# First token block in units of two feed-forward tiles, mean square of two blocks on VectorE, and a new load order, in a planned attention and feed-forward kernel

## The chip, the cores and the metric

The kernel runs on one core of one Trainium2 chip. The metric is the device time of one execution in microseconds (us).

## The reference

Attention with a window of 128 and four sink tokens over 4 batches x 8 heads x 768 positions x 64, and then, for the 3072 rows of 512 values, an RMS norm and a gated feed-forward layer of width 1536.

```python
def attention(q, k, v):                       # per batch and head
    scores = q @ k.T / sqrt(64)
    keep = (col < 4) | ((row - col >= 0) & (row - col < 128))
    a = softmax(where(keep, scores, -1e9))
    return a @ v

def ffn(x):                                   # x: 3072 x 512
    xn = x / sqrt(mean(x * x) + 1e-6) * rms_g
    g = xn @ w_gate                           # 512 x 1536
    return (g * sigmoid(g) * (xn @ w_val)) @ w_out
```

## The kernel before

The kernel works on 24 blocks of 128 tokens. A block passes through attention (transposes of q and k, scores, exponentials, masks, product with v), the RMS norm, and a transpose; four blocks form a group for the feed-forward layer, whose hidden width is cut into 12 tiles of 128 ("ft"). What is special here is that the program describes every operation with its needs, a priority and an estimated duration, and a small planner on the host (a list scheduler, run when the program is built) decides which engine's queue gets which operation next. Each engine then works through its own queue in that order and waits where a needed thing is not there yet.

```python
class Plan:
    LATE = 300
    def run(self):
        ...                                   # cut
        while left:                           # take the op that can start first,
            first = None                      # then the one of better priority
            for e, found in cand.items():
                for o in found:
                    ...                       # cut: ready time, PSUM banks
                    start = max(free[e], ready)
                    key = (start, o["prio"], ready, o["at"])
                    if first is None or key < first[0]:
                        first = key, e, o
            ...                               # cut: estimated end, DMA landing
            order.append((start, end, e, fn, o))
        return order
```

The settings that matter here: which loads go out in which order, how many of the first blocks get their mask from TensorE (as four matmuls of 512 columns that write a bias) and not from VectorE, from which block on the scores wait for a feed-forward unit (`GATE_FROM`), from which block on the loads wait for the scores of nine blocks earlier (`LEAD_FROM`), how many idle-time warm-up matmuls TensorE has, and how a group's columns and ft tiles are cut into units.

```python
    LOADS = "q-1 k-1 v-0 w-0-2 v-1 qkv-2 qkv-3 w-2-4 w-4-6 w-6-8 w-8-9 w-9-12 qkv-4 wo-0-6 qkv-5 wo-6-12 qkv-6 qkv-8 qkv-7"
    PE_MASKS = 2
    GATE_FROM = 6
    LEAD_FROM = 10
    WARM = 30
    CHUNKS = (4,2,2)                          # group 0: 4 column chunks, units of 4 ft
    GB_PRIO = 2000
    # ... cut
    def square(g):                            # ScalarE, with an accumulator
        ...
        nc.scalar.activation(out=sq, in_=x16, func=ACT.Square,
                             scale=1.0 / math.sqrt(DM), accum_out=T["ms", g])
    def rms(g):                               # VectorE, eight small operations
        m = small.tile([P, 1], FP32, name="m")
        nc.vector.tensor_scalar(out=m, in0=T.pop(("ms", g)), scalar1=1e-6, ..., op0=ALU.add)
        ...                                   # cut: 1/sqrt by iteration, then x * r * gb
    # ... cut
    for G in range(NG):
        for c in range(nc_):                  # token chunk
            for ft in range(0, FTN, nc_):     # nc_ ft tiles in a unit
                ffn(G, n, range(ft, ft + nc_), slice(c * w, (c + 1) * w), p0 + 10 * n)
    # ... cut
    order = plan.run()
    with tc.manual_schedule():
        for *_, fn, o in order:
            if fn is not None:
                fn()
```

The softmax here doesn't subtract the row's maximum and nothing guards it: scores larger than these inputs give would overflow.

Of the kernel before, what the change touches and what calls it, by code (L numbers as in the profile page):

```python
# [9 lines left out]
ALU = mybir.AluOpType  # L10
ACT = mybir.ActivationFunctionType
FP32 = mybir.dt.float32
BF16 = mybir.dt.bfloat16
I32 = mybir.dt.int32

P = 128
# [10 lines left out]
class Plan:  # L27
# [3 lines left out]


    LATE = 300
    HOP = {"PE": 40, "ACT": 35, "DVE": 35, "POOL": 90, "SP": 60}
    START = {"PE": 800, "ACT": 800, "DVE": 1030, "POOL": 1290, "SP": 800}

# [5 lines left out]
    def op(self, ways, needs=(), gives=(), prio=0.0, takes=(), drops=(), ring=None, work=0.0,  # L42
# [3 lines left out]
            drops=tuple(drops), ring=ring, work=work, mode=mode, at=len(self.ops), ready=0,  # L46
        ))

    def land(self, ring, first, work):


        r = self.rings
        if ring == "POOL":
            begin = max(first, r["POOL"], r["HW"])
            r["POOL"] = begin + (1.4 * work if begin < 8500 else work)
            self.loads -= 1
            return r["POOL"] + 520
        if ring == "HW":
            begin = max(first, r["HW"])
            r["HW"] = begin + (1.25 * work if begin > 2500 else work)  # L60
            return r["HW"] + 900
        begin = max(first, r["TR"], r["POOL"])
        if self.loads:
            r["POOL"] = max(r["POOL"], first) + work
            work *= 2
        r["TR"] = begin + work
        return r["TR"] + (350 if ring == "TR" else 650)

    def run(self):
        free, users = dict(self.START), {}  # L70
        self.loads = sum(o["ring"] == "POOL" for o in self.ops)
        wait = {o["at"]: set(o["needs"]) for o in self.ops}
        cand = {e: [] for e in free}
        left = len(self.ops)
        for o in self.ops:
            for t in o["needs"]:
                users.setdefault(t, []).append(o)
            if not o["needs"]:
                for e in o["ways"]:
                    cand[e].append(o)  # L80
        busy, warm, mode, order = [], False, 0, []
        while left:
            first = None
            for e, found in cand.items():
                for o in found:
                    k = len(o["takes"])
                    if k > len(self.banks):
                        continue
                    ready = o["ready"] + self.HOP[e] if o["ready"] else 0
                    if k:  # L90
                        ready = max(ready, sorted(self.banks.values())[k - 1] + 40)
                    start = max(free[e], ready)
                    key = (start, o["prio"], ready, o["at"])
                    if first is None or key < first[0]:
                        first = key, e, o
            if first is None:
                raise RuntimeError("stuck: %s" % [
                    (o["gives"], list(wait[o["at"]])) for o in self.ops if o["at"] in wait
                ][:20])
            (start, *_), e, o = first  # L100
            for x in o["ways"]:
                cand[x].remove(o)
            wait.pop(o["at"])
            left -= 1
            ns, lat, fn = o["ways"][e]
            if e == "PE":
                busy = [(a, d) for a, d in busy if a > start - 3413]
                warm = start - free[e] < 4000 and (warm or sum(d for a, d in busy) > 3000)
                ns = ns if warm else 2 * ns
                if o["mode"] != mode:  # L110
                    ns, mode = ns + 110, o["mode"]
                busy.append((start, ns if mode != 2 else 0))
                lat = ns + 180
            for s in o["takes"]:
                i = min(self.banks, key=lambda i: (self.banks[i], i))
                del self.banks[i]
                self.held[s] = i
            free[e] = start + ns
            end = start + lat
            if o["ring"] is not None:  # L120
                end = self.land(o["ring"], end, o["work"]) + self.LATE
            for s in o["drops"]:
                self.banks[self.held[s]] = end + 12
            for t in o["gives"]:
                for x in users.pop(t, ()):
                    x["ready"] = max(x["ready"], end + 12)
                    w = wait[x["at"]]
                    w.discard(t)
                    if not w:
                        for way in x["ways"]:  # L130
                            cand[way].append(x)
            order.append((start, end, e, fn, o))
        return order
# [3 lines left out]
def kernel(  # L137
# [13 lines left out]
    nc = tc.nc  # L151

    B, H, S, D = q.shape
    DM = H * D
# [8 lines left out]
    FTN = DFF // P  # L163
# [4 lines left out]
    HW = 4 * VW  # L168
# [3 lines left out]
    GROW = "SP"  # L172
    CAST_DVE = 600
    MASKS_PRIO = -5
    POOL_AT = (1,2)
    DEPTH = 8
    LOADS = "q-1 k-1 v-0 w-0-2 v-1 qkv-2 qkv-3 w-2-4 w-4-6 w-6-8 w-8-9 w-9-12 qkv-4 wo-0-6 qkv-5 wo-6-12 qkv-6 qkv-8 qkv-7"
    LOADS += "".join(f" qkv-{g}" for g in range(9, NB))
    PE_MASKS = 2
    POOL_MASK_FROM = 16  # L180
    X_DMA_FROM = 9
    QK_DMA_FROM = 8
    LD = 16
    GATE_FROM = 6
    LOAD_LEAD = 9
    LEAD_FROM = 10
    WARM = 30
    GATE_LEAD = 6
    T_LEAD = 3
    SPLIT = (0,1)  # L190
    CHUNKS = (4,2,2)
    GB_PRIO = 2000

    const = ctx.enter_context(tc.tile_pool(name="const", bufs=1))
    ld = ctx.enter_context(tc.tile_pool(name="ld", bufs=LD))
# [35 lines left out]
    T = {}  # L231
# [294 lines left out]
    def normal(g, u):  # L526
# [7 lines left out]
            in1=rden.unsqueeze(2).to_broadcast((P, 4, D)), op=ALU.mult,  # L534
        )

    def square(g):
        T["ms", g] = small.tile([P, 1], FP32, name="ms")
        sq = xpool.tile([P, DM], BF16, name="sq")
        nc.scalar.activation(  # L540
            out=sq, in_=T["x16", g].rearrange("p h d -> p (h d)"), func=ACT.Square,
            scale=1.0 / math.sqrt(DM), accum_out=T["ms", g],
        )

    def rms(g):
        m = small.tile([P, 1], FP32, name="m")
        nc.vector.tensor_scalar(
            out=m, in0=T.pop(("ms", g)), scalar1=1e-6, scalar2=None, op0=ALU.add,
        )
        y = small.tile([P, 1], FP32, name="y")  # L550
        nc.vector.tensor_scalar(
            out=y.bitcast(I32), in0=m.bitcast(I32), scalar1=-0.5,
# [94 lines left out]
    for g in range(NB):  # L647
# [41 lines left out]
        for u in range(2):  # L689
# [7 lines left out]
            else:  # L697
# [12 lines left out]
            dve(548, lambda g=g, u=u: normal(g, u),  # L710
                [("av", g, u)] + ([("xr", g - 3)] if g >= 3 else [])
                + ([("n", g - 1, u)] if g else []), [("n", g, u)], early, drops=[("av", g, u)])
        act(720, lambda g=g: square(g),
            [("n", g, 0), ("n", g, 1), "table"] + ([("ms", g - 1)] if g else []), [("ms", g)],
            early)
        dve(1745, lambda g=g: rms(g),
            [("ms", g), "gb"] + ([("xt", g - 3)] if g >= 3 else [])
            + ([("xr", g - 1)] if g else []), [("xr", g)], early)

        G = g // GB  # L720
# [32 lines left out]
    def mms(ps, w_sb, G, fts, cols):  # L753
        n = cols.stop - cols.start
        for i, ft in enumerate(fts):
            for kt in range(KTN):
# [2 lines left out]
                    rhs=T["xnt", G][:, kt, cols], start=(kt == 0), stop=(kt == KTN - 1),  # L759
                )  # L760

    def tanh(key):
        T["th", key] = spool.tile([P, 512], BF16, name="th")
        nc.scalar.activation(  # L764
            out=T["th", key], in_=BANK[("g", key)], func=ACT.Tanh, scale=0.5,
        )

    def silu(key):
        T["p1", key] = spool.tile([P, 512], BF16, name="p1")
        nc.vector.scalar_tensor_tensor(  # L770
            out=T["p1", key], in0=T.pop(("th", key)), scalar=1.0, in1=BANK.pop(("g", key)),
            op0=ALU.add, op1=ALU.mult,
        )

    def hidden(key, G, fts, cols):
        n, hk = len(fts), ("h", G, fts[0] // 4)
        if hk not in T:
            T[hk] = hpool.tile([P, 4, GN], BF16, name="hT")
        i = fts[0] % 4
        nc.vector.tensor_tensor(  # L780
            out=T[hk][:, i:i + n, cols],
            in0=T.pop(("p1", key)).rearrange("p (n c) -> p n c", n=n),
            in1=BANK.pop(("v", key)).rearrange("p (n c) -> p n c", n=n), op=ALU.mult,
        )

    def project(G, tb, i):
# [45 lines left out]
    def ffn(G, n, fts, cols, prio):  # L832
# [1 line left out]
        xs = [("xt", g) for g in range(G * GB + cols.start // P, G * GB + cols.stop // P)]  # L834
        before = [("h", keys[-3])] if len(keys) >= 3 else []
        keys.append(key)
        pe(864, lambda: mms(bank(("g", key)), wg, G, fts, cols),
           xs + [("wg", ft) for ft in fts], [("g", key)], prio, takes=[("g", key)])
        pe(864, lambda: mms(bank(("v", key)), wv, G, fts, cols),
           [("g", key)] + [("wv", ft) for ft in fts], [("u", key), ("F", G, n)], prio - 0.5,  # L840
           takes=[("v", key)])
        act(480, lambda: tanh(key), [("g", key), "table"] + before, [("th", key)])
        dve(600, lambda: silu(key), [("th", key)] + before, [("p1", key)], drops=[("g", key)])
        dve(605, lambda: hidden(key, G, fts, cols), [("p1", key), ("u", key)]
            + ([("O", G - 2, i) for i in range(GB)] if G >= 2 else []),
            [("h", key)], drops=[("v", key)])

    for G in range(NG):
# [1 line left out]
        nc_ = CHUNKS[G] if G < len(CHUNKS) else 1  # L850
        w, n = GN // nc_, 0
        for c in range(nc_):
            for ft in range(0, FTN, nc_):
                ffn(G, n, range(ft, ft + nc_), slice(c * w, (c + 1) * w), p0 + 10 * n)
                n += 1
        mine = [key for key in keys if key[0] == G]
        for tb in range(GB if G < NG - 1 else GB - 1):
# [61 lines left out]
```

## Time and profile before

| kernel before | |
|---|---|
| time, median of 3 | 246.89 us (246.82 to 247.07) |
| profiled execution | 245.98 us, span 244.3 us |
| TensorE busy | 232.6 us, 95% |
| VectorE / ScalarE busy | 183.7 / 131.2 us |

In the profile lines PE is TensorE (matmuls), PEld its weight loads, DVE VectorE, ACT ScalarE, POOL GpSimd and SP SyncE; L12 is line 12 of the kernel.

These are lines of the first two parts of the page of the kernel before: busy time of each engine, and the span in 40 slices (a digit is the busy share in tenths).

```profile
PE 232.6 (95%) x2098; PEld 147.8 (61%) x2120; DVE 183.7 (75%) x482; ACT 131.2 (54%) x276; POOL 88.8 (36%) x114
PE   4978999999999999999999999999999999999994
PEclk9999999999999999999999999999999999999999
DMA  8999999999999999999944544014311013200022
```

TensorE is full except in the first four slices, so TensorE bounds the kernel and only the start has idle TensorE time to give. DMA is full for the first half, because every q, k, v and weight has to come in.

The windows view of the kernel before gives busy time by engine for each stretch (start:end, length, then busy us and number of instructions of PE, PEld, DVE, ACT and POOL; then the granted TensorE clock, the DMA share and GB/s).

```profile
0.00:5.00 5.00, 1.88 (x11) 1.16 (x12) 2.59 (x16) 1.90 (x2) 3.79 (x10) 1.00 0.64 103
5.00:10.00 5.00, 4.45 (x35) 2.62 (x34) 0.99 (x3) 2.91 (x8) 5.00 (x7) 1.00 1.85 173
10.00:15.00 5.00, 4.12 (x63) 2.79 (x61) 4.01 (x16) 3.64 (x12) 5.00 (x7) 1.00 2.36 157
15.00:20.00 5.00, 3.58 (x62) 2.61 (x59) 4.46 (x16) 4.93 (x13) 3.31 (x6) 1.00 1.70 187
20.00:25.00 5.00, 4.81 (x92) 4.61 (x90) 4.29 (x12) 2.29 (x5) 3.33 (x5) 1.00 1.50 193
```

TensorE has 5.97 us idle in the first 20, almost nothing after that.

The timeline of TensorE of the kernel before (start, duration, what, and in brackets the idle time before it and what ended it):

```profile
4.16 1.87 PE L438 MATMUL s<-bias,idnos 128*128 128x512 bf16 x4 [2.07 <-DVE bias L273]
...
8.79 1.12 PE L399 MATMUL gb<-grow,ones 1*128 1x512 f32 x2
...
11.15 1.02 PE L438 MATMUL s<-bias,ident 128*128 128x512 bf16 x4
...
18.14 0.61 PE L757 MATMUL g<-xnt,wg 128*128 128x128 bf16 x8
19.75 0.62 PE L757 MATMUL g<-xnt,wg 128*128 128x128 bf16 x8 [1.00 <-DMA wg<-in_moe_w_gate_dram]
```

Three things are to be seen. Four mask matmuls of the same shape take 1.87 us at 4.16 and 1.02 us at 11.15, so TensorE runs at half its rate at first. The line PEclk shows 9 (of 10) throughout: it does not show this half rate. And the first feed-forward matmul comes at 18.14 and waits 1.00 us for the second gate load.

### The profile page before, as it was taken

The numbers are of one execution on the slowest core, as the hardware profiler recorded it, in microseconds if no ns is written. First come the engines' busy times: TensorE is split into PE (matmuls) and PEld (weight loads), VectorE is DVE, ScalarE is ACT, GpSimd is POOL, SyncE is SP. The second block draws the span as 40 slices with busy tenths as digits, with TensorE's granted clock in tenths as the row PEclk, the third lists the DMA queues.
The fourth block names the chain that finished last, engine by engine and source line by source line (L and its number), as shares of the span: only waits on it lengthen the run. The fifth ranks groups of instructions, "written<-read, shape, count | busy, mean of one in ns | idle before, by whom it ended". The sixth has DMA issues, their size and how long they took to land.

```text
span 244.3 us, 5510 instructions
## 1 busy us (share of the span) xinstructions
PE 232.6 (95%) x2098; PEld 147.8 (61%) x2120; DVE 183.7 (75%) x482; ACT 131.2 (54%) x276; POOL 88.8 (36%) x114
## 2 busy tenths in 40 slices
PE   4978999999999999999999999999999999999994
PEld 2557996875789765688875444444545544444443
DVE  4388979979899998899888499991299992377700
ACT  3886466778675837654537555735745521333111
POOL 8995755695444749423004200302504200000000
PEclk9999999999999999999999999999999999999999
DMA  8999999999999999999944544014311013200022
GB/s 112 172 170 195 192 188 188 156 146 174 171 196 130 156 124 179 142 216 133 149 35 107 133 107 86 3 21 108 120 34 21 4 21 107 86 3 0 0 86 86
DMA packets 111979, 27.22 MB, mean 111 GB/s; under 512 B 102097, under 2 KB 109009, under 8 KB 111954
## 3 DMA queue, kind: packets, MB, share of 16 engines
q0 software_dynamic: 80704, 13.90, 81.0%
q1 hardware_dynamic: 31106, 12.85, 27.0%
q8 instruction: 16, 0.26, 0.5%
q10 hardware_dynamic: 144, 0.13, 0.2%
q14 instruction: 9, 0.07, 0.1%
HBM read 28.31 MB, written 6.29 MB: 142 GB/s over the span
## 4 chain that ended last, share of the span: by engine, by line
PE 77%; DVE 9%; POOL 5%; DMA 4%; issue 3%; ACT 0%; POOLq 0%; DVEq 0%; ACTq 0%
PE o L790 23%; PE g L757 21%; PE v L757 21%; PE s L456 4%; DMA wg<-in_moe_w_gate_dram 4%; DVE hT L780 2%; PE av L520 2%; DVE p L770 2%; PE av L515 2%; DVE r L560 2%; POOL v L327 1%; DVE xr L564 1%; PE av L505 1%; PE o_last L808 1%; DVE x L532 1%
## 5 line engine op out<-in xcount | busy, mean ns | idle before, releaser
L757 PE MATMUL g<-xnt,wg 128*128 128x128 bf16 (+2 forms) x525 | 69.8, 282 | 1.6 <-DMA wg<-in_moe_w_gate_dram 1.2
L757 PE MATMUL v<-xnt,wv 128*128 128x128 bf16 (+2 forms) x522 | 71.0, 281 | 0.3
L764 ACT ACTIVATE th<-g 128x512 bf16<-128x512 f32 x72 | 42.9, 600 | 46.7 <-PE g L757 45.2
L790 PE MATMUL o<-wo,hT 128*128 128x512 bf16 x263 | 62.6, 379 | 1.2 <-issue 0.6
L770 DVE SCALAR_TENSOR_TENSOR p<-th,g 128x512 bf16<-128x512 bf16 x72 | 48.1, 683 | 16.6 <-ACT th L764 16.2
L757 PEld LDWEIGHTS <-wg 128*128 128x128 bf16 x528 | 43.1, 98 | 21.0 <-DMA wg<-in_moe_w_gate_dram 1.5
L757 PEld LDWEIGHTS <-wv 128*128 128x128 bf16 x528 | 42.6, 98 | 18.5 <-issue 0.8
L469 ACT ACTIVATE e<-s 128x512 bf16<-128x512 f32 (+1 forms) x104 | 48.4, 542 | 6.6 <-PE s L456 6.3
L780 DVE TENSOR_TENSOR hT<-p,v 128x512 bf16<-128x512 bf16 x72 | 47.2, 682 | 1.5 <-PE v L757 0.6
L790 PEld LDWEIGHTS <-hT 128*128 128x128 bf16 x276 | 25.6, 98 | 28.7 <-issue 1.3
L491 POOL TENSOR_SCALAR_AFFINE_SELECT e<-e 128x512 bf16<-128x512 bf16 x14 | 9.4, 680 | 61.8 <-ACT e L469 48.8
L798 ACT ACTIVATE osb<-o 128x512 f32<-128x512 f32 x23 | 13.8, 599 | 29.0 <-PE o L790 29.0
L323 POOL DMA_DIRECT2D k<-in_k_dram x23 | 20.5, 890 | 15.9 <-DMA v<-in_v_dram 7.0
L323 POOL DMA_DIRECT2D q<-in_q_dram x23 | 20.5, 893 | 13.0 <-DMA k<-in_k_dram 3.8
L327 POOL DMA_DIRECT2D v<-in_v_dram x24 | 21.3, 889 | 10.0 <-DMA q<-in_q_dram 6.0
L532 DVE TENSOR_TENSOR x<-av,rden 128x256 bf16<-128x256 f32 x48 | 20.4, 425 | 1.7
L540 ACT ACTIVATE sq<-x 128x512 bf16<-128x512 bf16 x24 | 15.2, 632 | 9.4 <-DVE x L532 9.3
L531 DVE RECIPROCAL rden<-av 128x4 f32<-128x4 f32 x48 | 8.5, 177 | 15.4 <-PE av L520 15.3
L486 DVE TENSOR_TENSOR e<-e,masks 128x1024 bf16<-128x1024 bf16 (+1 forms) x30 | 18.9, 650 | 1.0 <-ACT e L469 0.8
L564 DVE SCALAR_TENSOR_TENSOR xr<-x,r,gb 128x512 bf16<-128x512 bf16 x24 | 19.0, 790 | 0.9
L520 PE MATMUL av<-v,e 128*128 128x65 bf16 x192 | 16.9, 194 | 0.0
L515 PE MATMUL av<-v,e 128*128 128x65 bf16 x160 | 15.0, 193 | 0.0
(70 smaller groups left out, 177.2 us busy)
## 6 DMA issues: line engine op xcount, KB each, us to landing
out_dram<-osb SPq DMA_DIRECT2D x23, 256.0 KB, 2.2
v<-in_v_dram POOLq DMA_DIRECT2D x24, 128.0 KB, 10.4
q<-in_q_dram POOLq DMA_DIRECT2D x23, 128.0 KB, 10.9
k<-in_k_dram POOLq DMA_DIRECT2D x23, 128.0 KB, 10.8
wo<-in_moe_w_out_dram POOLq DMA_DIRECT2D x2, 768.0 KB, 12.0
wg<-in_moe_w_gate_dram POOLq DMA_DIRECT2D x4, 256.0 KB, 7.8
wv<-in_moe_w_val_dram POOLq DMA_DIRECT2D x4, 256.0 KB, 8.2
wg<-in_moe_w_gate_dram POOLq DMA_DIRECT2D x1, 384.0 KB, 9.4
```

The source lines that it names most:

```text
L323: nc.gpsimd.dma_start(out=T[name, g], in_=block_of(src, g))
L327: nc.gpsimd.dma_start(out=V16[b][:, t, :, 0:D], in_=block_of(v, g))
L469: nc.scalar.activation(out=T["e", g, u][:, 2 * hi:2 * hi + 2, n0:n1, :].rearrange("p x n c -> p x (n c)"), in_=ps.rearrange("p (j c) -> p ...
L515: nc.tensor.matmul(out=dest, lhsT=T["e", g - 1, u][:, x, 1, :], rhs=V16[b][:, t - 1, h, :], start=(t == 1), stop=False, skip_group_check=True,
L520: nc.tensor.matmul(out=dest, lhsT=T["e", g, u][:, x, 0, :], rhs=V16[b][:, t, h, :], start=(t == 0), stop=True, skip_group_check=True,)
L532: nc.vector.tensor_tensor(out=T["x16", g][:, 4 * u:4 * u + 4, :], in0=pvv[:, :, 0:D], in1=rden.unsqueeze(2).to_broadcast((P, 4, D)), op=AL ...
L564: nc.vector.scalar_tensor_tensor(out=T["xr", g], in0=T.pop(("x16", g)).rearrange("p h d -> p (h d)"), scalar=r[:, 3:4], in1=gb, op0=ALU.mu ...
L757: nc.tensor.matmul(out=ps[:, i * n:(i + 1) * n], lhsT=w_sb[:, kt, ft * P:(ft + 1) * P], rhs=T["xnt", G][:, kt, cols], start=(kt == 0), sto ...
L764: nc.scalar.activation(out=T["th", key], in_=BANK[("g", key)], func=ACT.Tanh, scale=0.5,)
L770: nc.vector.scalar_tensor_tensor(out=T["p1", key], in0=T.pop(("th", key)), scalar=1.0, in1=BANK.pop(("g", key)), op0=ALU.add, op1=ALU.mult,)
L780: nc.vector.tensor_tensor(out=T[hk][:, i:i + n, cols], in0=T.pop(("p1", key)).rearrange("p (n c) -> p n c", n=n), in1=BANK.pop(("v", key)) ...
L790: nc.tensor.matmul(out=BANK[("o", G, tb)], lhsT=T["h", G, ft // 4][:, ft % 4, tb * P:(tb + 1) * P], rhs=wo[:, ft, :], start=(ft == 0), sto ...
```

## The change

The intent is to let feed-forward work start earlier: the first token block works in units of two ft tiles, so that it needs only one pair of weight loads to begin; weights for ft 2-3 come before ft 0-1; both after the q, k, v of blocks 1 to 3; and the mean square plus eps of the first two blocks is one VectorE operation with an accumulator, where ScalarE's Square, its accumulator read and a VectorE addition were three. The diff also changes the planner's model of the DMA, and several settings. This is its core; cut are the planner's internals (a new landing model, a slack of 0) and the code for tiles of another size.

```diff
-    POOL_AT = (1,2)
+    POOL_AT = (0,1)
-    LOADS = "q-1 k-1 v-0 w-0-2 v-1 qkv-2 qkv-3 w-2-4 w-4-6 w-6-8 w-8-9 w-9-12 qkv-4 wo-0-6 qkv-5 wo-6-12 qkv-6 qkv-8 qkv-7"
+    LOADS = "q-1 k-1 v-0 v-1 qkv-2 qkv-3 w-2-4 w-0-2 w-4-6 w-6-9 w-9-10 w-11-12 w-10-11 qkv-4 wo-0-6 qkv-5 wo-6-12 qkv-8 qkv-7 qkv-6"
-    PE_MASKS = 2
+    PE_MASKS = 3
-    GATE_FROM = 6
+    GATE_FROM = 7
-    LEAD_FROM = 10
-    WARM = 30
+    LEAD_FROM = 9
+    WARM = 0
-    SPLIT = (0,1)
+    SPLIT = (0,2)
+    FIRST = 2
+    SQ2 = 0
+    SQD = 2
-    GB_PRIO = 2000
+    GB_PRIO = -970
 ... (cut)
     def rms(g):
         m = small.tile([P, 1], FP32, name="m")
+        if g < SQD:
+            sq = xpool.tile([P, DM], BF16, name="sq")
+            nc.vector.tensor_tensor_reduce(
+                out=sq, in0=x16, in1=x16, scale=1.0 / DM, scalar=1e-6, op0=ALU.mult,
+                op1=ALU.add, accum_out=m,
+            )
 ... (cut)
         for c in range(nc_):
-            for ft in range(0, FTN, nc_):
-                ffn(G, n, range(ft, ft + nc_), slice(c * w, (c + 1) * w), p0 + 10 * n)
+            k = min(nc_, FIRST) if G == 0 and c == 0 else nc_
+            for ft in range(0, FTN, k):
+                ffn(G, n, range(ft, ft + k), slice(c * w, (c + 1) * w), p0 + 10 * n)
```

## The prediction

> **What bounds the kernel now.** TensorE. The page gives it 232.6 of 244.3 us (95%); the windows view gives 4.81 of 5 us for 20 to 25 us, and after that at least 19.2 in every 20 us until the last evacuation at 240.85. The late DVE stretch of the chain (176 to 203 us) is no bound: the timeline shows matmuls back to back there. So only the first 20 us can give much: there TensorE is idle 5.97 us (windows: 1.88, 4.45, 4.12, 3.58 busy), part of its busy time is 30 warm-up matmuls or runs at half rate (four 512-column mask matmuls take 1.87 us at 4.16 us, 1.02 at 11.15), and the first feed-forward matmul comes at 18.14, stops after 8, and waits 1.0 us for the second gate load, landing at 19.7. From 10.6 to 20.7 us DVE is nearly full as well.
>
> **What changes, beyond the title.** (1) The first weight pair now follows the loads of blocks 1 to 3, and the pair for ft 2-3 comes first. By the issue view the first pair holds up later loads by about 1.3 us in queue (4.7 to 6.0 us from issue to landing) and 1.4 us of issue; without it, q, k and v of blocks 2 and 3 land about 2.6 us earlier (q of block 2 near 10.4, not 12.96), gate ft 2-3 near 17, ft 0-1 near 19 to 19.7, ft 4-5 as now (22). (2) The first token block runs in two-ft units, so it starts on one pair: about 0.9 us of matmuls at 17 to 18.5. Cost: three more units, about 3 x 2 x 70 ns fixed on DVE. (3) Square on ACT (0.63 + 0.19 accumulator read) and the DVE add (0.15) become one DVE operation for blocks 0 and 1. My estimate, from the 512-wide two-tensor operations here (0.68 to 0.79): 0.7 us plus a short accumulator read. The Trainium skill ("VectorE: DVE Perf Modes", Two Vector instructions with no wait between them) says an operation that also writes its accumulator is two instructions; no run here shows that for DVE yet. It saves 0.2 to 0.4 us of latency per block, costs DVE 0.6, frees ACT 0.65. (4) Block 2 is masked by TensorE: +0.9 us TensorE (in idle time), -1.28 us DVE. (5) No warm-up matmuls, gain-broadcast matmul early, split scores on block 2 rather than 1, other gates: small.
>
> **On the critical path.** Useful TensorE work that moves ahead of 20 us is gained one to one, since TensorE is full afterwards. I count 0.5 us of feed-forward and 1 to 2 us of attention (blocks 2 and 3), less what DVE, still full, doesn't let through (net DVE change about -0.1 us), and less a possible gap at 23 to 25 us, when only ft 0-5 have landed and the new three-ft load is due near 25. Net gain 1 to 3 us.
>
> **Predicted: 245.0 us, range 242.8 to 247.2.** Chances: faster by over 2% 0.07, within 2% 0.90, slower 0.03.
>
> **What would show it.** First feed-forward matmul near 17 us; q of block 2 transposed near 10.5; the last FFN weights still landing near 31; from 25 us on, TensorE full and later stages simply 1 to 3 us earlier; the accumulator operation 0.65 to 0.85 us; DVE total within 1 us of 183.7; ACT about 1 us less.
>
> **What would make it wrong.** TensorE at half rate longer without the warm-ups (over 1 us lost); longer starvation for weights at 21 to 27 us; x of block 1 or 2 later because DVE carries the squares; or the reshuffled later schedule opening TensorE idle after 40 us. A gain above 5 us would mean idle time after 25 us that I don't see.

## The result, and the profile after

| | median | range | n |
|---|---|---|---|
| before | 246.98 us | 246.82 to 247.17 | 4 |
| after | 247.72 us | 247.39 to 248.28 | 4 |

The ratio is 1.0032 with an interval of 1.0010 to 1.0054: the same at the 2% mark, but slower, not faster, and above the predicted range (242.8 to 247.2). Later, eleven runs of before against six unaltered runs of after gave 1.0052 (1.0035 to 1.0069): about 1 us is lost.

The same lines of the page of the kernel after (profiled at 248.28 us, the slowest of its runs):

```profile
PE 233.7 (95%) x2072; PEld 147.0 (60%) x2094; DVE 184.2 (75%) x484; ACT 131.0 (53%) x278; POOL 89.5 (36%) x116
PE   5986999989999999999999899999999999999994
```

The slices show less idle time in the first three, but a 6 in the fourth slice (18.5 to 24.6 us), where before had an 8, and an 8 in the slices around 52 and 138 us, where before had only nines. The windows and the timeline of TensorE of the kernel after say what they are:

```profile
15.00:20.00 5.00, 4.19 (x70) 3.00 (x69) 4.64 (x18) 4.64 (x15) 3.77 (x6) 1.00 1.46 199
20.00:25.00 5.00, 3.44 (x64) 3.12 (x63) 3.42 (x12) 1.91 (x6) 2.23 (x3) 1.00 1.37 199
```

```profile
9.79 1.67 PE L462 MATMUL s<-bias,ident 128*128 128x512 bf16 x4
...
17.52 0.62 PE L813 MATMUL g<-xnt,wg 128*128 128x128 bf16 x8
...
22.24 0.62 PE L813 MATMUL g<-xnt,wg 128*128 128x128 bf16 x8 [1.05 <-DMA wg<-in_moe_w_gate_dram]
22.70 0.39 PE L626 MATMUL x<-ident,xr 128*128 128x128 bf16 x4
23.59 0.62 PE L813 MATMUL v<-xnt,wv 128*128 128x128 bf16 x8 [0.51 <-DMA wv<-in_moe_w_val_dram]
...
53.09 0.40 PE L440 MATMUL k<-ident,k 128*128 128x128 bf16 x4 [0.78 <-DVE r L607]
...
139.10 1.02 PE L813 MATMUL g<-xnt,wg 128*128 128x512 bf16 x4 [0.85 <-DMA xnt<-xr]
```

The first feed-forward matmul does come earlier (17.52). But at 22 us TensorE waits for the weights of ft 4-5, and since its queue is fixed, the transpose of block 1 (ready since about 20.4 us, when its last VectorE operation ended) stands behind that wait. Two more waits appear late, of 0.78 us before 53 us and of 0.85 us before 139 us, the second at the seam where the feed-forward work passes from group 2 to group 3.

### Which execution of before to compare with

The profile of before was one of its good executions. Both kernels were run again unaltered.

> The kernel before once more, unaltered: a ratio of 1.000 within 0.002, and a second profile. If the first profile was an unusually good execution (its 245.98 us is below all timed runs), the second shows TensorE at half rate well beyond 8.5 us, x of block 0 copied later than 14.9 us by 1 us or more, and useful matmul work at 24 us lower by 1 us or more. If it was typical, the second is like it within 0.3 us.

> The changed kernel once more, unaltered, so that the edits are compared with it in the same rounds, not with its four first runs, the kernel before having ranged from 246.67 to 247.02 us in median over the batches. Every account expects 247.4 to 248.3 us, a ratio to before of 1.003 to 1.006. If it comes out above 1.006, the edits run so far were compared with too low a value.

The unaltered before took 247.11 us (245.48 to 247.28, 4 runs, ratio 1.0002), its profile 247.08. The unaltered after took 247.80 us (247.70 to 248.71, 6 runs). The waits of 1.05 and 0.85 us are in the second profile of after too, the one of 0.78 us is not:

```profile
22.36 0.62 PE L813 MATMUL g<-xnt,wg 128*128 128x128 bf16 x8 [1.10 <-DMA wg<-in_moe_w_gate_dram]
...
138.55 1.02 PE L813 MATMUL g<-xnt,wg 128*128 128x512 bf16 x4 [0.85 <-DVE y L598]
```

The timeline of TensorE of the second profile of before:

```profile
9.46 2.07 PE L399 MATMUL gb<-grow,ones 1*128 1x512 f32 x2
...
13.39 1.91 PE L438 MATMUL s<-bias,ident 128*128 128x512 bf16 x4
...
20.58 1.06 PE L757 MATMUL g<-xnt,wg 128*128 128x128 bf16 x16
```

Here the gain broadcast takes 2.07 us (1.12 in the first profile) and the masks 1.91 (1.02): in this execution TensorE stayed at half rate until about 16.5 us, in the first one only until about 8.4. The first feed-forward matmul came at 20.58, not 18.14. Two other profiles with before's start (below: the square in before, and the VectorE delay) show the slow start too, with masks of 1.91 us at 13.2 and 13.6. So the start that the prediction read was the exception among four.

The measure used from here on is **useful matmul work by time**: the matmuls that started by then, counted by shape, each times its full-rate pitch as read from back-to-back starts in the trace (0.056 us for 128 columns, 0.109 for 256, 0.216 for 512, and so on); masks, warm-ups and the gain broadcast are left out. Up to 0.2 us of it can be a missing record: the totals at the end are 219.8 for before and after, but 220.0 for e19 and e20.

| by (us) | before, 2nd profile | after, 2nd profile | difference | e19 (below) minus before | e20 (below) minus before |
|---|---|---|---|---|---|
| 20 | 4.83 | 6.67 | +1.84 | +1.78 | +1.78 |
| 24 | 8.06 | 8.96 | +0.90 | +1.06 | +1.62 |
| 30 | 14.11 | 14.89 | +0.78 | +1.06 | +1.06 |
| 60 | 42.86 | 43.07 | +0.21 | +0.43 | +0.43 |
| 120 | 101.43 | 101.54 | +0.11 | +0.66 | +0.55 |
| 142 | 122.83 | 122.18 | -0.65 | +0.65 | +0.65 |
| 235 | 213.06 | 212.85 | -0.21 | +1.30 | +1.08 |

One row is too good: the score matmuls of 64 rows start in pairs and those of the sink tokens in fours, 3 to 4 ns apart, and the count gives them more than the group takes. Counted at what the group takes, the lead at 20 us is 1.51 (1.45 for e19 and e20); from 24 us on no difference of the table changes.

The predicted gain of 1 to 3 us at the start did come (+1.5 to +1.84 at 20 us), against a usual execution of before. It was given back in three places: 0.6 to 0.9 us at 20 to 24 (weights), 0.6 at 30 to 60, and 0.8 at 120 to 142 (the seam). The first two profiles, whose before is the good execution, lose in the same stretches: after minus before is +0.78 at 20 us, -1.06 at 24, -0.78 at 30, -1.86 at 60, -1.75 at 120 and -2.30 at 142. This pair of profiles differs by 0.6 us in time and by 0.2 us in span, less than the mean 1 us; so the table shows where the gain goes, not the whole mean difference.

### The profile page after: what moved, and what is told of

It reads as the page before. It is cut to its first block, busy times and chain, and to the rows that moved or that the text cites. A ratio compares the mean times of both kernels' runs of the same rounds, so it can differ in the third digit from the quotient of the medians.

```text
span 246.2 us, 5472 instructions
## 1 busy us (share of the span) xinstructions
PE 233.7 (95%) x2072; PEld 147.0 (60%) x2094; DVE 184.2 (75%) x484; ACT 131.0 (53%) x278; POOL 89.5 (36%) x116
## 4 chain that ended last, share of the span: by engine, by line
PE 81%; DVE 6%; DMA 5%; POOL 5%; ACT 2%; issue 1%
PE v L813 25%; PE g L813 25%; PE o L852 20%; DMA wv<-in_moe_w_val_dram 4%; PE s L480 4%; PE av L544 2%; PE av L539 1%; POOL v L351 1%; DVE r L607 1%; PE av L529 1%; PE o_last L870 1%; DVE xr L611 1%; POOL k L347 1%; DVE x L556 1%; DMA xnt<-xr 1%
## 5 line engine op out<-in xcount | busy, mean ns | idle before, releaser
L824 ACT ACTIVATE th<-g 128x512 bf16<-128x512 f32 (+1 forms) x75 | 43.4, 588 | 51.3 <-PE g L813 51.0
L852 PE MATMUL o<-wo,hT 128*128 128x512 bf16 x263 | 63.3, 379 | 0.8 <-issue 0.3
L831 DVE SCALAR_TENSOR_TENSOR p<-th,g 128x512 bf16<-128x512 bf16 (+1 forms) x75 | 48.3, 661 | 16.5 <-ACT th L824 16.2
L841 DVE TENSOR_TENSOR hT<-p,v 128x512 bf16<-128x512 bf16 (+1 forms) x75 | 47.4, 660 | 2.0 <-PE v L813 1.3
L515 POOL TENSOR_SCALAR_AFFINE_SELECT e<-e 128x512 bf16<-128x512 bf16 x14 | 8.8, 633 | 63.9 <-ACT e L493 34.3
L556 DVE TENSOR_TENSOR x<-av,rden 128x256 bf16<-128x256 f32 x48 | 20.4, 425 | 1.7
L510 DVE TENSOR_TENSOR e<-e,masks 128x1024 bf16<-128x1024 bf16 (+1 forms) x28 | 17.6, 648 | 1.4 <-ACT e L493 1.4
L574 ACT ACTIVATE sq<-x 128x512 bf16<-128x512 bf16 x22 | 13.9, 634 | 7.6 <-DVE x L556 7.3
L544 PE MATMUL av<-v,e 128*128 128x65 bf16 x192 | 16.8, 193 | 0.0
L544 PEld LDWEIGHTS <-e 128*128 128x128 bf16 x192 | 13.1, 98 | 2.6 <-ACT e L493 0.3
## 6 DMA issues: line engine op xcount, KB each, us to landing
v<-in_v_dram POOLq DMA_DIRECT2D x24, 128.0 KB, 10.5
wg<-in_moe_w_gate_dram POOLq DMA_DIRECT2D x1, 384.0 KB, 10.5
```

The lines of the kernel that those rows point to most:

```text
L510: nc.vector.tensor_tensor(out=ev, in0=ev, in1=mv, op=ALU.mult)
L544: nc.tensor.matmul(out=dest, lhsT=T["e", g, u][:, x, 0, :], rhs=V16[b][:, t, h, :], start=(t == 0), stop=True, skip_group_check=True,)
L556: nc.vector.tensor_tensor(out=T["x16", g][:, 4 * u:4 * u + 4, :], in0=pvv[:, :, 0:D], in1=rden.unsqueeze(2).to_broadcast((P, 4, D)), op=AL ...
L824: nc.scalar.activation(out=T["th", key], in_=BANK[("g", key)][:, 0:n], func=ACT.Tanh, scale=0.5,)
L831: nc.vector.scalar_tensor_tensor(out=T["p1", key], in0=T.pop(("th", key)), scalar=1.0, in1=BANK.pop(("g", key))[:, 0:n], op0=ALU.add, op1= ...
L841: nc.vector.tensor_tensor(out=T[hk][:, i:i + n, cols], in0=T.pop(("p1", key)).rearrange("p (n c) -> p n c", n=n), in1=BANK.pop(("v", key)) ...
```

## The experiments

Theories. **A:** the new start is better, and the order that the planner made for the rest loses it again. **B:** a single wait (for weights at 22, for k at 53, or for x at 139) costs the time, and taking it away brings the time down by as much. **C:** the start is slack, so that neither gain nor loss there reaches the end. **D:** the missing warm-up matmuls keep TensorE at half rate longer. Most edits reorder the finished list of operations just before it is emitted (`move` puts the named ones behind or before another), so that nothing else moves; the data flow stays as it was. All runs gave the right result.

### The square by itself

Before with the VectorE square for its first two blocks, and after with ScalarE's square again:

```diff
 # e5_dvesq_in_before, in rms of before, for g < 2 (square does nothing there):
-    nc.vector.tensor_scalar(... 1e-6 ... add)
+    nc.vector.tensor_tensor_reduce(... accum_out=m)
 # e4_actsq, in rms of after, for g < SQD:
-    nc.vector.tensor_tensor_reduce(... accum_out=m)
+    square(g); nc.vector.tensor_scalar(... 1e-6 ... add)
```

> The kernel before with one edit: mean square plus eps of blocks 0 and 1 in one DVE operation, all queues otherwise in the order of before. Theory A: x of block 0 comes 0.2 to 0.4 us earlier, of block 1 within 0.3 us; total within 0.3 us of the kernel before, since the second gate load lands at 19.7 us in any case. Rival B (full DVE): slower by 0.5 us. Rival C: faster by 0.5 us.

> The changed kernel with the two DVE squares given back to ScalarE (Square, then the DVE add), every queue otherwise in the changed order. Theory A (the DVE operation shortens the chain of block 0 and 1 but the weights set the pace, so it is worth nothing in the total): x of block 0 comes 0.2 to 0.8 us later, because ScalarE is busy with copies and exps there, and the time moves by less than 0.3 us. Rival B (the DVE squares hurt, DVE being nearly full from 12 to 22 us): 0.5 us or more faster with ScalarE. Rival C (they help): 0.5 us or more slower.

Measured: 246.69 us, ratio 1.0006 (0.9992 to 1.0020) in before; 247.42 us, 1.0031 (1.0014 to 1.0049) in after without it. So the square on VectorE is worth nothing that can be seen in the total, either way. Its parts were sized well. The VectorE groups of the kernel after, from 12 to 22 us (count, then busy us and mean ns):

```profile
L585 DVE CUSTOM_DVE_ANT_0 sq<-x 128x512 bf16<-128x512 bf16 x2 | 1.4, 687 | 0.0
L585 DVE DVE_READ_ACCUMULATOR2_ANT m<- 128x1 f32 x2 | 0.2, 82 | 0.0
```

It is two instructions, as the Trainium skill says of an operation that writes its accumulator ("VectorE: DVE Perf Modes", Two Vector instructions with no wait between them); here 0.69 and 0.08 us. From the end of the last normalised half of block 0 to the start of its final VectorE scaling it is 1.96 us in after and 2.35 us in e4_actsq: 0.39 us of latency saved, as was estimated. In e5 the saving does not even reach the copy of x of block 0: it comes at 17.33 us, against 17.34 in the second profile of before.

### Is the start slack?

Before, with four VectorE memsets (1.9 us by the groups view) in front of the norm of block 0:

```diff
 def rms(g):
+    if g == 0:
+        for _ in range(4):
+            nc.vector.memset(dummy, 0.0)      # 128 x 512 fp32
```

> The kernel before with about 2.3 us of useless DVE memsets between the normalisation and the rms of block 0, all queues otherwise unchanged: x of blocks 0 and 1 come about 2 us later. The prediction's claim (TensorE is full after 20 us, so what is earlier or later before that counts one to one): the time rises by 1.5 to 2.3 us. Theory A (the weights' transfer sets the pace up to about 27 us, so readiness of x in the start has slack): it rises by less than 0.8 us.

249.24 us against 247.02, ratio 1.0085 (1.0071 to 1.0099). The timeline of ScalarE, first of this run and then of the second profile of before, shows the copy of x of blocks 0 and 1:

```profile
19.26 0.58 ACT L589 COPY xnt<-x 128x512 bf16<-128x512 bf16 x1 [2.04 <-PE x L583]
24.59 0.66 ACT L589 COPY xnt<-x 128x512 bf16<-128x512 bf16 x1
```

```profile
17.34 0.58 ACT L585 COPY xnt<-x 128x512 bf16<-128x512 bf16 x1 [0.36 <-PE x L579]
22.67 0.66 ACT L585 COPY xnt<-x 128x512 bf16<-128x512 bf16 x1
```

Both copies are 1.92 us later and the kernel takes 2.2 us more (difference of the medians). This delay of the start, with the order kept, costs about one to one, so C falls. The two profiles of before show the same for a gain, with no edit at all: the first is ahead of the second by 1.51 us of useful work at 30 us, still by 1.08 at 235, and its time is 1.10 us lower. So in before's order most of what the start gives or takes reaches the end; whether it does in after's order is what the next runs ask.

### Taking the wait for weights away

After, with the unit of ft 4-5 of token block 0 (five operations on three engines) queued after block 1's first unit:

```diff
 order = plan.run()
+order = move([(n, (0, 4, 0)) for n in ("g", "th", "p1", "u", "h")], after=("u", (0, 0, 128)))
```

> The changed kernel with one edit: five operations (gate and value matmuls, tanh, and both DVE products of ft 4-5 for token block 0) are queued after block 1's first unit, not before it. All else keeps its order on every queue. Theory A (TensorE stands behind the weights of ft 4-5 while block 1 is ready behind it): block 1's transposes move from 22.7 to about 21, the waits of 1.05 and 0.51 us for those weights shrink by at least 1 us together, and the useful matmul work done by 26 us rises by 0.4 to 1.0 us; time 0.3 to 0.9 us below the changed kernel's 247.7. Rival B (the transfers bind: the next load, gate of ft 6-8, lands only at 25.4, so the wait is only moved): TensorE waits near 24.5 to 25.4 for it, and the time moves by under 0.2 us.

247.74 us, 1.0047 (1.0029 to 1.0065): not faster than after. The waits view of TensorE (us in total, times, longest) no longer has the gate weights in it; in their place stand

```profile
PE g L813 <- DVE x L556: 0.7, 1, 0.7
PE v L813 <- DMA wv<-in_moe_w_val_dram: 0.5, 2, 0.3
```

The wait of 0.70 is for the copy of x of block 1 (put down to the VectorE operation before it). Useful work by 24 us is 9.91 (after: 8.96), but by 60 it is 43.07, the same as after. B falls for this wait: what it gives by 24 us is mostly gone by 30 (a lead over before of 1.12 us, 0.78 in after) and all gone by 60.

Units of four for the first block again, planned anew:

```diff
-    FIRST = 2
+    FIRST = 4
```

> The changed kernel with units of four ft tiles for the first token block too (the list of operations is scheduled anew, so later stages can shift as well). Theory A (two-ft units do let feed-forward start earlier, but the gain is gone by 26 us): useful matmul work at 20 us is about 0.5 us lower, at 26 us the same within 0.4 us, and the time within 0.7 us of the changed kernel. Rival B (the smaller units are what costs): 0.7 us or more faster. Rival C (they gain): 0.7 us or more slower.

248.34 us, 1.0064 (1.0047 to 1.0082). Work by 20 us is 6.22 (after: 6.67), but by 60 it is 43.14 (43.07). The two-ft units give 0.45 us at 20 us, which has no weight by 60. The total does not isolate them, since planning anew changed later stages too: this run loses 1.6 us against before between 60 and 80 us, where after loses 0.2. The difference to after's 1.0052 on another chip is within the intervals.

### The loads of blocks 6 to 8

After loads them as 8, 7, 6, and k of block 6 lands near 53 us. Two other orders in the same nine places:

```diff
+loads of the slots of (8, 7, 6): now (6, 8, 7)    # e2_load6;  e3_both: this and e1_fill
+loads of the slots of (8, 7, 6): now (7, 6, 8)    # e9_load768
```

> The changed kernel with one edit: in the three load slots 8, 7, 6 the blocks are loaded as 6, 8, 7 (the kernel before has that order). Theory A (the wait of 0.78 us at 52.3 us, which the profile puts down to a DVE operation, is really k of block 6 landing at about 53): that wait goes, k of block 6 lands about 8 us earlier, and the time falls by 0.6 to 1.2 us, to about 246.8. Rival B (DVE or a bank is what holds the transposes of block 6): the wait stays and the time moves by under 0.2 us.

> Both edits of the two runs before this one. If the two waits are separate losses, the gains add: 0.9 to 1.8 us below the changed kernel, about 246.0 to 246.8, so faster than the kernel before (246.98). If they only move the same slack, it is no faster than the better of the two.

> The changed kernel with one edit: the three load slots 8, 7, 6 carry blocks 7, 6, 8. This is the order in which the changed kernel's TensorE queue transposes them (7 before 6), which the earlier try with 6, 8, 7 ignored. Theory A (the wait of 0.78 us at 52.3 us is k of block 6 landing just then): the wait goes and useful matmul work at 60 us rises by 0.6 to 1.1 us; time 0.4 to 1.1 us below the changed kernel. Rival B (something on DVE holds the transposes): the wait stays, time within 0.2 us.

250.06, 250.84 and 248.25 us (ratios 1.0147, 1.0151 and 1.0064). The first two were badly designed: TensorE's queue in after transposes block 7 before block 6, so with 6, 8, 7 it was q of block 7 that came last. The waits of TensorE in e2_load6 and in e9_load768:

```profile
PE q L440 <- DMA q<-in_q_dram: 2.8, 1, 2.8
```

```profile
PE s L480 <- DMA qkT<-q: 0.7, 1, 0.7
```

In e9 the wait of 0.78 at 53 us is gone, and one of 0.72 at 58 us, for block 8, is new. The wait moved. Besides, the second profile of after had no wait at 53 us at all and lost 0.57 us against before from 30 to 60 us all the same, so this wait is not the whole cause.

### The seam at 138 us

After, with the first gate unit of group 3 and its tanh moved behind the projections of group 2 (e13); the seam's TensorE order made like before's, as far as single moves can (e17); and combinations:

```diff
+order = move([("g", (3, 0, 0)), ("th", (3, 0, 0))], after=("po", 2, 3, 2))           # e13_g3
+order = move([("kp", 6), ("kT", 6)], before=("s", 6, 0))                             # e15_three: with e1's and e13's
+order = move([("ss", 2, 2)], before=("po", 2, 0, 1))                                 # e17_avs: these two with e13's,
+order = move([("po", 2, 0, 2), ("osb", 2, 0), ("st", 2, 0)], after=("av", 15, 1))    # e18_fill_avs: with e1's too
```

> The changed kernel with one edit: the first gate unit of token group 3 and its tanh are queued after the last two output matmul groups of token group 2, as the kernel before has them, not before. Theory A (TensorE stands for 0.85 us at 138 us behind x of block 15 while eight output matmuls, 1.7 us, lie ready behind it): the wait goes and the time falls by 0.5 to 0.9 us, to 246.8 to 247.2. Rival B (the chain through x of block 15 ends the stretch in any order): the wait moves to a later instruction, time within 0.3 us.

> The changed kernel with all three queue-order edits: ft 4-5 of token block 0 behind block 1's first unit; k of block 6 transposed just before its scores, not 1.8 us of ready matmuls earlier; the first unit of group 3 behind the outputs of group 2. Theory A (the change lost its gain in three places where an in-order TensorE queue stands at its head for a transfer, with ready work behind): all three waits shrink by 0.8 us or more, 0.28 or more and 0.8 us, and the time falls by 1.0 to 2.0 us, to 245.7 to 246.7, at or below the kernel before. Rival B (the gain was never there, transfers and the chains behind them set the time): under 0.6 us.

> The changed kernel with the order of the kernel before at the seam between token groups 2 and 3: sink scores first, av of blocks 14 and 15 before the last output matmuls of block 8, and the first unit of group 3 behind the outputs of group 2. Theory A (the stage of 120 to 200 us costs the changed kernel 1.0 us of useful matmul work because the chain av, normalisation, rms, transposing transfer of blocks 14 and 15 starts 0.9 us later in the queue): DVE gets to blocks 14 and 15 about 0.9 us earlier relative to TensorE's work, the work done from 120 to 200 us rises from 76.9 to about 77.7, and the time is 0.5 to 1.0 us below the changed kernel of the same rounds. Rival B (the loss there is not this order): within 0.3 us.

> The run before plus the edit at the start (ft 4-5 of token block 0 behind block 1's first unit, work at 26 us then equal to the kernel before). Theory A (start and seam are two separate losses that add): 0.8 to 1.6 us below the changed kernel, at or below the kernel before. Rival B (what the start wins is lost again at the seam): no faster than the seam edit alone.

248.80 (1.0070), 248.46 (1.0059), 248.91 (1.0088) and 248.75 us (1.0087). All are no better than after (1.0032 to 1.0052). In e13 the wait of 0.85 us is gone, and these are new in TensorE's waits:

```profile
PE av L544 <- DVE e L510: 0.3, 1, 0.3
PE av L544 <- POOL e L515: 0.2, 1, 0.2
```

Its work by 142 us is 122.62 (after, second profile: 122.18), but by 160 it is 138.69 (139.53). B falls here too. A wait that one queue shows is where the orders of all queues meet; moving one operation in one or two queues makes them meet elsewhere.

### The half rate at the start

After with 18 warm-up matmuls in front, and after with the gain broadcast late as in before:

```diff
+for _ in range(18):                              # e6_warm: first in TensorE's queue
+    nc.tensor.matmul(out=wps[:, 0:P], lhsT=zeros, rhs=zeros, start=True, stop=True)
```

```diff
+late = [order[at[n]] for n in ("gbm", "gb")]     # e12_gb_late: gain broadcast put
+# ... inserted before the operation that gives ("vs", 0, 0)
```

> The changed kernel with 18 warm-up matmuls on zeros put in front of TensorE's queue (idle there until 3.07 us); nothing else changes order. Theory A (the half rate until about 11 us delays block 0, whose x is copied at 16.3 rather than 14.9 us): the mask matmuls of block 1 take about 1.0 rather than 1.67 us, the gain broadcast 1.1 rather than 2.07, x of block 0 comes 0.7 to 1.4 us earlier. Of the total at most 0.3 us comes back, because the first weights land at 15.85 and 18.5 us and x of block 1 stands behind the weights of ft 4-5. Rival B (the early half rate is what ate the expected gain): the time falls by 0.8 us or more.

> The changed kernel with the gain broadcast (one 1-row float32 matmul and its copy) moved from 5.3 us to just after block 0's av matmuls. Theory A (a 2 us stretch of a 1-row matmul does not count as activity, and it is why TensorE stays at half rate to about 11.5 us where the kernel before is at full rate by 8.5): the mask matmuls of block 1 take about 1.0 rather than 1.7 to 1.9 us and x of block 0 comes about 0.7 us earlier; total moves less than 0.4 us. Rival B (the half rate has another cause, as 18 warm-ups in front did not end it): the mask matmuls stay at 1.7 to 1.9 us.

247.91 us (1.0077, 1.0035 to 1.0120; two of six runs 250.5 and 250.7) and 248.48 us (1.0068, 1.0052 to 1.0085). The timeline of TensorE with the warm-ups:

```profile
1.06 2.10 PE L952 MATMUL wps<-zeros 128*128 128x128 bf16 x18 [1.06 <-DVE zeros L949]
...
9.70 1.89 PE L462 MATMUL s<-bias,ident 128*128 128x512 bf16 x4
...
12.63 0.58 PE L440 MATMUL q<-ident,q 128*128 128x128 bf16 x4 [0.17 <-DVE rden L555]
...
13.56 0.41 PE L440 MATMUL q<-ident,q 128*128 128x128 bf16 x4
```

TensorE was busy 2.94 of 3 us from 1 to 4 us and all of the next six by the windows view, and still ran at half rate: the masks at 9.70 take 1.89 us, and the transposes of one q reach 0.41 us, from 0.58, only at 13.56. D falls: more work in front did not bring the full rate earlier. In e12 the masks of block 1, at 9.81, still took 1.70 us (1.67 in after), so the early broadcast is not what keeps the half rate. The broadcast, now at 11.79, took 1.12 us, so TensorE was at full rate there, but the masks at 16.25 took 1.91: it fell back. When the full rate comes was not under the control of any edit here.

### The same start with the later settings of before

The last pair keeps after's start and plans all queues anew, with three settings of before that act only later. From 124 to 144 us its plan for TensorE is before's, operation for operation. The traces bear this out: by tile and shape, TensorE's order in e19 is after's up to 45 us, and before's from 53 to 112 us and from 124 us to the end.

```diff
-    GATE_FROM = 7
-    LEAD_FROM = 9
-    LOADS = "... wo-6-12 qkv-8 qkv-7 qkv-6"
+    GATE_FROM = 6
+    LEAD_FROM = 10
+    LOADS = "... wo-6-12 qkv-6 qkv-8 qkv-7"
 # e20_late_before_fill: and e1_fill's move
```

> The kernel after, planned anew with three of the later settings of the kernel before (gate from block 6, load lead from block 10, last loads in the order 6, 8, 7). Its planned start to 44 us is that of the kernel after, its planned seam of token groups 2 and 3 that of the kernel before, operation for operation. Theory (the start gains, two later stages of the new order give it back): the work ahead at 24 to 30 us stays at +0.8 to 0.9, the loss of 0.5 at 40 to 60 us and of 0.7 at 120 to 142 us does not come, and the time is 246.0 to 246.7, 0.3 to 1.0 under the kernel before. Rival (TensorE time gained early is lost later whatever the order, because DVE is the limit around 140 to 200 us): 247.2 to 247.9, as the kernel after.

> The same, and besides the unit of ft 4-5 of token block 0 moved after the first unit of token block 1, as in e1_fill. If the wait for weights at 21 to 24 us costs the whole anything once the later stages no longer do, 0.2 to 0.6 under e19; if not, the same as e19 within 0.3.

e19 took 246.61 us (246.38 to 246.96), ratio 0.9994 (0.9979 to 1.0009); e20 took 246.14 us (245.79 to 247.01), ratio 0.9977 (0.9960 to 0.9994); before was 246.94 in the same rounds. So e19 wins back about 1.1 us on after (0.9 to 1.4 by the ratios to before; after itself was not run in these rounds), and e20 is the fastest kernel, 0.2% faster than before with an interval that leaves out 1. The windows view from 135 to 140 us, in this order: second profile of before, second profile of after, e19:

```profile
135.00:140.00 5.00, 4.75 (x43) 2.46 (x43) 2.50 (x11) 2.82 (x8) 2.06 (x4) 1.00 0.66 144
```

```profile
135.00:140.00 5.00, 4.10 (x38) 2.04 (x36) 3.86 (x12) 3.17 (x9) 1.55 (x3) 1.00 0.50 146
```

```profile
135.00:140.00 5.00, 4.95 (x44) 2.46 (x43) 2.66 (x11) 3.01 (x8) 1.74 (x3) 1.00 0.60 167
```

TensorE (first number) loses 0.90 us there in after and nothing in e19. In the table above e19 keeps its lead of 0.65 through the seam (+0.66 at 120, +0.65 at 142), where after loses 0.76. This is what A said, and its rival (the time is lost later under any order) expected about 247.2 to 247.9. VectorE has less to do in this stretch in e19 and before (2.66 and 2.50 us) than in after (3.86); whether that is why the single moves failed was not tested.

A does not hold everywhere. At 30 to 60 us e19 loses as much as after (from +1.06 to +0.43), though its load order is before's. The windows from 40 to 45 us, second profile of before and then e19, show why in part (the fourth busy number is ScalarE):

```profile
40.00:45.00 5.00, 4.95 (x59) 2.89 (x59) 4.53 (x15) 4.00 (x9) 2.26 (x4) 1.00 1.79 183
```

```profile
40.00:45.00 5.00, 4.72 (x50) 2.51 (x49) 4.26 (x14) 5.00 (x14) 2.59 (x4) 1.00 1.73 186
```

ScalarE is full in e19 (after: 4.98), and TensorE idles 0.28 us, where before has 4.00 and 0.05. That ScalarE is what holds TensorE there is a reading of these lines; no run took ScalarE work away.

The move of e1_fill gave nothing in after. In e20 it gives 0.47 us over e19 by the medians; the intervals overlap, so this is likely but not settled.

## Why the prediction was wrong

- **What bounds the kernel:** right. That start time counts in full is right in before's order: a VectorE delay whose x copies came 1.92 us late cost 2.2 us.
- **The start:** mostly right. First feed-forward matmul near 17 predicted, 17.52 and 17.83 measured; the last value load was issued at 23.83 us and landed 7.95 us later, near 32, where 31 was predicted. q of block 2 was transposed about 12.4, not 10.5: the data had landed at 10.65 (issued at 5.35), but TensorE worked on blocks 0 and 1 until about 12.3. Useful work at 20 us was ahead by 1.5 to 1.84 us of a usual execution of before; predicted were 1 to 3.
- **The profile of before was taken for a usual execution:** a hidden assumption that was wrong. It was 0.9 us faster than the median, with TensorE at full rate at 8.4 us. Against that profile the lead at 20 us is only 0.78 (6.78 against 6.00).
- **Costs of the square:** right. 0.69 and 0.08 us (0.7 and a short read), latency saved 0.39 and, for block 1, 0.22 us (0.2 to 0.4). VectorE 184.2 us (within 1 of 183.7). ScalarE about 1 us less was wrong: 131.0 against 131.2. In the total it is worth nothing visible (1.0006).
- **The step that failed:** "Useful TensorE work that moves ahead of 20 us is gained one to one", and with it "from 25 us on, TensorE full and later stages simply 1 to 3 us earlier". Already by 24 us 0.6 to 0.9 us of the lead was gone, by the wait for ft 4-5 that the prediction had as a risk ("a possible gap at 23 to 25 us", "longer starvation for weights"). Later stages then ran in another order, because the planner had made all queues anew: 0.6 us went at 30 to 60 us and 0.8 at the seam of groups 2 and 3. The prediction named this as a risk ("the reshuffled later schedule opening TensorE idle after 40 us") and gave it no size. e19 shows what it was worth: the same start with a later schedule planned from before's settings takes 246.61 us, about 1.1 less than after. Even there most of the lead at 20 us is lost by 60 us (+0.43 left), and the time is no more than 0.3 us below before.
- **Warm-ups:** the risk "TensorE at half rate longer without the warm-ups" did not come against a usual execution of before (against the profile that the prediction read it did: 11 us, not 8.4). Warm-ups in front did not shorten the half rate, and before's start, which has them, was at half rate longer in three of its four profiles.

Still open: which of the three later settings makes the seam good; why single moves in after could not; what ends the half rate; and what takes the 0.6 us at 30 to 60 us (0.47 of it between 40 and 44 us, in the second profile of after). The pair of profiles also shows less than the mean difference between the two kernels.

## What to carry to other kernels

When a change runs a scheduler anew, compare useful matmul work of both kernels at several times, and not only the stage that was meant: a gain at the start is only worth what the new order of the last stages leaves of it, and it pays to combine the new start with the old later settings. Taking away one long wait in a program with fixed queues mostly moved it here. Planning all queues again with other settings helped (e19, e20), but it is no cure by itself: e7, planned anew, lost 1.6 us in a stretch that its edit was not meant for. Before trusting a start that a profile shows, look whether its execution is as fast as the timed ones, and look at equal matmuls for a half rate that the clock line doesn't show.

## What the Trainium skill lacked or had wrong

- "TensorE: Matmul & The Clock Gate", Part 1: The HAM clock gate, has the array at half clock until it has been busy for about 3.4 us, and says that the point varies from run to run. The rates agree with these traces (four 512-column matmuls in 1.87 or 1.02 us). The time doesn't, if all that the profile counts as busy counts: with warm-ups in front TensorE was busy from 1.06 us with almost no gap (2.94 of 3 us, then 6.00 of 6) and stayed at half rate until about 13.5 us. Only the first 3.7 us of it are warm-ups and masks. The same program, before, switched near 8.4 us in one execution and near 16.5 in another. The copy of x of block 0 came at 14.90 us in the one and at 17.34 in the other; 0.4 us of that was there before either switched (q transposed at 7.01 and 7.42), which leaves 2.0. The section calls the penalty "<1% of a typical kernel span". That holds, 2.0 of 245 us being 0.8%, but it is larger than all that was at stake here.
- The same page, Part 4: PE-mode transpose, says that transposes don't count as busy in the same way. It may be the reason, or part of it, since this start is full of transposes; no run here separates it.
- The same page: that a kernel falls back to half rate in the midst of busy work was seen in e12_gb_late (broadcast at full rate, 1.12 us at 11.79; masks at half rate, 1.91 us at 16.25). The section HAM oscillation names idle gaps of more than about 3.4 us for this; the longest wait between the two here was 0.69 us, so that is not the reason. The page also tells of many short idle times as a cause, so it does not lack the case; no run here shows whether it is this one.
- No page gives the cost of this VectorE operation with an accumulator: 0.69 us for 512 bf16 columns, and 0.08 us for its accumulator read. "VectorE: DVE Perf Modes" has 691 ns for a plain fp32 add of two tensors with 512 columns, which fits the first.
